# An attention and MLP kernel on one core: slots 1 to 24 by a new order table, with clock-holding matmuls, slots 8 and 9 turned by DMA, and the first hidden units computed part by part

## The chip, the cores and the metric

The kernel runs on one core of a Trainium2 chip. The metric is the device time of one execution in microseconds; lower is better. The engines are named as in the profile: PE is TensorE, with its weight loads as PEld; DVE is VectorE, ACT is ScalarE, POOL is GpSimd, and SP is SyncE, which here only issues DMAs.

## What is computed

```python
# q, k, v: (8, 8, 576, 64) float32; w_in: (512, 2048); w_out: (2048, 512)
scores = q @ k.T / sqrt(64)                       # per batch and head, 576 x 576
kth    = the 32nd largest score of each row
attn   = softmax(where(scores >= kth, scores, -1e9))
x      = (attn @ v) with heads side by side       # 4608 x 512
h      = x @ w_in
out    = (h * sigmoid(1.702 * h)) @ w_out         # 4608 x 512
```

So each of 4608 rows per head pair needs its 32 largest scores, a softmax over these, and the product with v; then each of the 4608 tokens goes through an MLP with 2048 hidden values.

## The kernel before, in words

**Slots.** The work is cut into 144 slots (list `slots`, eighteen for each of eight batches). A slot is 128 rows of queries for a pair of heads; the last 64 rows of two pairs share a slot. Batch 0 has slots 0 to 17: slots 0 to 3 are the four head pairs of the first 128 rows, slots 4 to 7 those of the next, and so on. When the four pairs of one set of rows are through, they make a *block* of 128 tokens for the MLP. For a slot n the steps are:

- PE multiplies queries and keys into PSUM (`scores`, tile s_ps), two slots ahead; there is one set of score banks. ACT copies them out (`copy_scores`, tile sc).
- DVE pairs the two halves of each row as maximum and minimum (`pair_up`, tile ranked), one slot ahead, and finds the 32 largest by four rounds of eight, taking each eight out before the next (`topk`, `find`, tiles top and ranked).
- POOL makes the thresholds (`bounds`, tiles cut and low); ACT masks and exponentiates (`mask`, `exps`, tile pr); POOL and DVE invert the sums (`invert`, tiles some and rden).
- The weights are turned so that the keys lie on partitions (tile pt). In slots 0 to 9 PE does it: POOL scales an identity by the inverse sums (`divide`, tile by), PE multiplies by it in eight full matmuls and two half ones (`turn_main`, `turn_ends`, tile tp), and ACT copies PSUM out in two copies of 128x512 and one of 128x128. From slot 10 on a DMA does it: POOL scales the weights themselves (`normalize`), ACT splits them into 16-bit halves (`split`), SP writes them to DRAM (rows) and reads them back transposed (`turn_by_dma`).
- PE multiplies by v (`values`, later `values_at` and `values_of_two`, tile o), and ACT puts the result in its place in the block (tile xT).

**The MLP.** The 2048 hidden values of a block are cut into four *units* of 512. `hidden` computes one in PSUM: four groups of 128 by four steps of 128 over x, 16 matmuls, where step c needs head pair c of the block. The tile is one of two banks (po) or a borrowed one (ph). `tanh` and `gate` make the activation on ACT and POOL, and `project` multiplies it by w_out into the two banks. The first two blocks are computed whole; the later ones by a Strassen scheme.

**Weights.** 32 pieces of w_in and w_out are loaded by SP into a ring of seven places (`load_piece`, tile raws), and rounded in slots 0 to 10 (`round_piece`): some steps on ACT, a shift on DVE, and a last addition on POOL that frees the place. `may_project` asks whether the pieces that a projection needs have been finished; in slot n those of the slots before n have, which are 3n − 1 pieces. A projection of unit u of a block needs 16 + 4u.

**The order.** `slot(n)` issues slots 0 to 10, `filling_slot(n)` slots 11 to 20, and `steady_pair(n)` pairs of slots from 21 on. The steps of everything up to slot 24 are collected and then issued in the order of a table, `ORDER`, a permutation of their numbers written out in the file (`issue_in_order`; "8 11 0+8" means steps 8, 11 and 0 to 7). Each engine takes its steps strictly in that order. From slot 25 on the steps are issued as the code has them. In the profile a step out of the table has line 133 (L133), one behind it line 131 (L131), since every engine call goes through the helper `Engine`.

**Around the change.** `stay_warm(count)` (line 282) issues matmuls of the identity on itself whose result nobody reads. In slots 1 to 3, as long as no block is ready, `slot` ends with eight of these. The first block is complete when slot 3's values are in place; `bring_all` (line 1050), called in slot 5, brings them and issues the first unit, and `hidden` at the end of slots 5, 6 and 7 the other three. From slot 8 on `slot` projects one unit at its end if more than two wait and their weights are there. Slots n from 4 on turn slot n − 1 at their end and multiply it by v at once.

Of the kernel before, what the change touches and what calls it, by code (L numbers as in the profile page):

```python
# [19 lines left out]
P = 128  # L20
# [125 lines left out]
def kernel(  # L146
# [43 lines left out]

    FIRST = (TAIL, 0)
    MAIN = (0, NF + 1)
    SCALE = 1.0 / float(D) ** 0.5


    PROJECTS = 7


    TURNS = 4
    SETTLED = 10  # L200
    PAIRED = SETTLED + 1
    STEADY = PAIRED + 2
# [1214 lines left out]
```

## Time and profile before

| | |
|---|---|
| median of 3 runs | 1366.73 us |
| lowest and highest | 1366.28, 1373.02 us |
| the profiled execution | 1371.88 us |
| its span, first to last instruction | 1370.1 us |
| mean granted TensorE clock | 0.995 |
| busy: PE, DVE, ACT, POOL | 1340.9, 1274.6, 1166.2, 978.4 us |

The profile is of one execution. The span is shorter than that execution by 1.8 us around it. A busy engine is one that has an instruction in flight; for PE the ends of matmuls are modelled, and a matmul in 32-bit floating point shows as two records. The idle time before an instruction is put down to what released it last. The DVE and PE are called late or early here by the time at which they issue their first step behind the table.

### The profile page before, as it was taken

What the parts mean: (1) busy time and instruction counts of PE and PEld (TensorE: products, weight loads), DVE (VectorE), ACT (ScalarE), POOL (GpSimd) and SP (SyncE); (2) the same over time, 40 slices, a digit from 0 to 9 for tenths busy, and PEclk for the clock granted to TensorE, in tenths of its full rate; (3) what the DMA queues carried; (4) which work ended last, traced back from release to release, by engine and by line L of the source; (5) the groups of instructions that cost most, each with busy time, mean ns of one, the idle gap of its engine ahead of it and who ended that gap; (6) DMA issues with size and microseconds to landing.
All of it is one profiled execution on the core that took longest, in us unless ns stands there. A gap on an engine that the chain in (4) does not pass through costs nothing.

```text
span 1370.1 us, 54342 instructions
## 1 busy us (share of the span) xinstructions
PE 1340.9 (98%) x22532; PEld 1202.3 (88%) x22532; DVE 1274.6 (93%) x3374; ACT 1166.2 (85%) x1936; POOL 978.4 (71%) x1782
## 2 busy tenths in 40 slices
PE   7899999999999999999999999999999999999998
PEld 5687588999989998999999999999998999999998
DVE  7999999999999999999999999999999999999912
ACT  6999898998889979898889888998988888888841
POOL 3888887777767776777777777777777777777770
PEclk9899999999999999999999999999999999999999
DMA  8443759677998767988899796988899767765540
GB/s 233 144 146 110 177 155 212 170 191 195 217 211 212 183 150 203 209 200 197 206 208 206 181 195 164 237 192 196 204 202 202 192 172 181 186 148 135 143 122 17
DMA packets 527223, 246.92 MB, mean 180 GB/s; under 512 B 458880, under 2 KB 505472, under 8 KB 526976
## 3 DMA queue, kind: packets, MB, share of 16 engines
q1 hardware_dynamic: 526544, 243.16, 72.9%
q8 instruction: 177, 2.90, 0.9%
q14 instruction: 70, 0.57, 0.1%
q10 hardware_dynamic: 432, 0.30, 0.1%
HBM read 46.01 MB, written 103.42 MB: 109 GB/s over the span
## 4 chain that ended last, share of the span: by engine, by line
PE 86%; DMA 4%; DVE 3%; ACT 3%; POOL 1%; SPq 1%; issue 1%; DVEq 0%; ACTq 0%; POOLq 0%
PE ph L131 31%; PE po L131 28%; PE o L131 10%; PE s_ps L131 9%; PE po L133 4%; DMA pt<-rows 2%; DVE ranked L133 2%; PE o L133 1%; DVE top L133 1%; PE s_ps L133 1%; SPq L131 1%; PE ph L133 1%; PE tp L133 1%; ACT sc L133 1%; DMA rows<-sc 1%
## 5 line engine op out<-in xcount | busy, mean ns | idle before, releaser
L131 DVE MAX8 top<-ranked 128x8 f32<-128x288 f32 (+1 forms) x952 | 526.7, 595 | 0.0
L131 PE MATMUL ph<-xT,win 128*64 128x128 f32 x8064 | 464.2, 273 | 0.0
L131 PEld LDWEIGHTS ph<-xT,win 128*64 128x64 f32 x8064 | 441.2, 137 | 25.9 <-issue 21.9
L131 DVE MATCH_REPLACE8 ranked<-top,ranked 128x288 f32<-128x288 f32 x714 | 382.0, 543 | 0.0
L131 ACT COPY sc<-pr 128x2304 uint16<-128x2304 uint16 x120 | 253.7, 2114 | 87.0 <-POOL pr L131 87.0
L131 POOL TENSOR_SCALAR pr<-pr,rden 128x576 f32<-128x576 f32 x240 | 177.3, 749 | 40.0 <-DVE rden L131 40.0
L131 PE MATMUL po<-wout,h 128*64 128x128 f32 x2000 | 194.2, 273 | 0.0
L131 PE MATMUL po<-raws,h 128*64 128x128 f32 x2000 | 194.2, 273 | 0.0
L131 ACT ACTIVATE pr<-sc,low 128x576 f32<-128x576 f32 x240 | 183.4, 770 | 0.2 <-POOL raws L131 0.2
L131 POOL TENSOR_SCALAR some<-den 128x2 f32<-128x2 f32 x120 | 26.7, 222 | 209.8 <-ACT pr L131 209.8
L131 ACT ACTIVATE sc<-sc,cut 128x576 f32<-128x576 f32 x240 | 174.1, 781 | 0.1
L131 DVE TENSOR_TENSOR ranked<-s_ps,sc 128x576 f32<-128x576 f32 x236 | 166.6, 747 | 4.3 <-ACT sc L131 4.3
L131 POOL TENSOR_TENSOR th<-th,h 128x512 f32<-128x512 f32 x123 | 157.7, 1282 | 10.3
L131 PE MATMUL po<-wout,th 128*64 128x128 f32 x2064 | 156.6, 273 | 0.0
L131 ACT COPY sc<-s_ps 128x576 f32<-128x576 f32 x234 | 138.0, 642 | 19.8 <-PE s_ps L131 9.7
L131 PE MATMUL s_ps<-qk_t 64*64 64x288 f32 x1872 | 140.5, 415 | 0.0
L131 PEld LDWEIGHTS po<-wout,h 128*64 128x64 f32 x2000 | 126.4, 137 | 0.0
L131 PEld LDWEIGHTS po<-raws,h 128*64 128x64 f32 x2000 | 126.4, 137 | 0.0
L131 PEld LDWEIGHTS po<-wout,th 128*64 128x64 f32 x2064 | 121.3, 137 | 0.0
L131 PE MATMUL o<-pt,v_l 128*64 128x128 f32 (+1 forms) x2144 | 120.7, 266 | 0.0
L131 PEld LDWEIGHTS o<-pt,v_l 128*64 128x64 f32 x2144 | 106.6, 137 | 9.9 <-issue 9.1
L131 POOL TENSOR_TENSOR h<-th 128x128 f32<-128x128 f32 x248 | 114.1, 460 | 0.3
(121 smaller groups left out, 2216.6 us busy)
## 6 DMA issues: line engine op xcount, KB each, us to landing
rows<-sc SPq DMA_DIRECT2D x134, 576.0 KB, 3.8
qk_rows<-halves SPq DMA_DIRECT2D x24, 576.0 KB, 5.2
out_dram<-raws SPq DMA_DIRECT2D x68, 128.0 KB, 3.6
raws<-in_moe_w_in_dram SPq DMA_DIRECT2D x16, 512.0 KB, 4.7
raws<-in_moe_w_out_dram SPq DMA_DIRECT2D x16, 512.0 KB, 3.7
qk_l<-in_q_dram SPq DMA_DIRECT2D x28, 256.0 KB, 4.2
qk_l<-in_k_dram SPq DMA_DIRECT2D x28, 256.0 KB, 4.4
v_l<-in_v_dram SPq DMA_DIRECT2D x4, 1024.0 KB, 7.5
```

Source lines behind the costliest of these rows:

```text
L131: do(*args, **kwargs)
L133: self.engines.collected.append(lambda: do(*args, **kwargs))
```

## The change

Slots 1 to 3 get three matmuls of `stay_warm` at four places each (slots 2 and 3 at five), in place of eight at the end. Slots 8 and 9 are turned by DMA, as the slots from 10 on are; their values are multiplied one slot later, in slots 10 and 11. The first block's first two units are done part by part: the steps over x of head pairs 0 and 1 at the end of slot 3, into the two banks, and those of head pairs 2 and 3 in slot 5. The block's third and fourth unit follow in slots 5 and 6. Slot 6 gets a second `tanh` and `gate`. Projecting begins in slot 7, and no longer asks for more than two units waiting. The table is new from its first line to its last.

```diff
@@ -33,89 +33,89 @@
 ORDER = """
-8 11 0+8 9 12 10 13+5 22 18 23+2 33 25+2 19 27+5 34 32 20 38+4 35 21 36 97 37 42+4 98 46+4 99 50 54+6 100 53 51
...
-2592 2514+2 2528+2 2516+2 2530+4 2518+6 2534+2 2585+2
+8 11 0+8 9 12 10 13+5 22 18 23+2 33 25 19 26+5 20 31 34 32 21 38+4 97 35+3 98 42+8 99 50 54+2 100 56+4 53 51
...
+2532+2 2583+2
 """
...
@@ -193,10 +193,11 @@
     SCALE = 1.0 / float(D) ** 0.5
 
 
-    PROJECTS = 7
+    PROJECTS = 6
 
 
     TURNS = 4
+    BY_DMA = 8
     SETTLED = 10
     PAIRED = SETTLED + 1
     STEADY = PAIRED + 2
@@ -284,6 +285,10 @@
         none = both_banks[1][:]
         for i in range(count):
             nc.tensor.matmul(none[:, 0:P], lhsT=of, rhs=of, start=True, stop=True)
+
+    def warm(n):
+        if 0 < n < TURNS:
+            stay_warm(3)
 
     def load(name, b, hp, queue=None):
 
@@ -1047,6 +1052,29 @@
 
     put_off = []
 
+    def hidden_part(c, place):
+
+        for g in range(2):
+            for i in range(G):
+                nc.tensor.matmul(
+                    both_banks[g][:, i * P : (i + 1) * P],
+                    lhsT=win[:, c, (g * G + i) * P : (g * G + i + 1) * P],
+                    rhs=xs[:, place, c, :],
+                    start=(c == 0 and i == 0),
+                    stop=(c == CC - 1 and i == G - 1),
+                )
+
+    def bring_parts():
+
+        while put_off:
+            put_off.pop(0)()
+        x = ready[0]
+        for c in range(2, CC):
+            hidden_part(c, x.place)
+        for bank in both_banks:
+            fs, x.left = x.left[:G], x.left[G:]
+            to_gate.append((bank[:], fs, x))
+
     def bring_all():
 
         waiting = len(ready)
@@ -1078,14 +1106,16 @@
         else:
             exponentials(n - 1, bring_all if n % 4 == 1 and n > TURNS + 1 else lambda: None)
             if n == TURNS + 1:
-                pass
-                bring_all()
+                bring_parts()
             copy_scores(n + 1)
             bring_all()
             if 1 < n <= TURNS:
                 turn_main(n - 2)
                 turn_ends(n - 2)
+                warm(n)
             if n > TURNS + 1:
+                tanh(True)
+            if n == TURNS + 2:
                 tanh(True)
             do("size", 3)
             if n == TURNS + 1:
@@ -1099,7 +1129,9 @@
                 if last and n > 2:
                     last["pool_size"]()
             if i == (9 if n < 3 else 7):
-                if n > 0:
+                if n > BY_DMA:
+                    invert(n - 1)
+                elif n > 0:
                     divide(n - 1)
                 if last and n < 3:
                     last["pool_size"]()
@@ -1114,13 +1146,21 @@
                 do("shift", 3)
             if i == (13 if n == TURNS + 1 else 10):
                 gate()
+            if i == 13 and n == TURNS + 2:
+                gate()
+            if i in (2, 6, 11):
+                warm(n)
         bounds(n)
         for piece in some:
             unfinished.extend(piece["finish"][piece is last :])
         if n < NP:
             for fn, args in preparing:
                 fn(*args)
-        if n >= TURNS:
+        if n > BY_DMA:
+            normalize(n - 1)
+            split(n - 1)
+            turn_by_dma(n - 1)
+        elif n >= TURNS:
             turn_main(n - 1)
             turn_ends(n - 1)
         do("low", 3)
@@ -1131,21 +1171,22 @@
             copy_scores(n + 2)
         if n == 0:
             return
-        idle = not ready and n < TURNS
+        warm(n)
         if 1 < n <= TURNS:
             values(n - 2, put_off if n == TURNS else None)
-        if n >= TURNS:
-            values(n - 1, put_off)
+        if n == TURNS - 1:
+            for c in range(2):
+                hidden_part(c, place_of(0, 0))
+        if n >= TURNS and n != BY_DMA + 1:
+            values(n - 2 if n > BY_DMA else n - 1, put_off)
         if n >= NP:
             for fn, args in preparing:
                 fn(*args)
-        if n > PROJECTS and may_project(2):
+        if n > PROJECTS and may_project(0):
             project(n == SETTLED)
-        if idle:
-            stay_warm(8)
         if n == SETTLED:
             turn_qk(1, 0)
-        hidden()
+        hidden(ps_t if n == TURNS + 1 else None)
 
     def dues(n):
 
@@ -1247,7 +1288,7 @@
         unit = lambda: hidden(ps_t)
         th = lambda: tanh(True)
         sums = lambda count: lambda: sum_weights(count)
-        put = lambda: project(True)
+        put = lambda: project(True) if to_project else None
         held = lambda n: lambda: brought.append(values_held(n))
         bring = lambda: brought.pop(0)()
 
@@ -1265,10 +1306,10 @@
 
         gate()
         bring_all()
-        filling_slot(11, [copy_qk], [], [unit], [])
+        filling_slot(11, [copy_qk], [], [lambda: values(BY_DMA + 1, put_off), unit], [])
         finish_all()
         summing.extend(all_weight_sums())
-        filling_slot(12, [th], [sums(1)], [put, put, ends_in_turn], [])
+        filling_slot(12, [bring_all, th], [sums(1)], [put, put, ends_in_turn], [])
         filling_slot(13, [copy_ends, th, leave_all], [gate, sums(1)], [of_qk(1), put, held(13)], [sums(1)])
         filling_slot(14, [copy_qk, bring], [gate, sums(1)], [put, hidden], [sums(1)])
         filling_slot(15, [copy_ends, th], [sums(3)], [put, hidden, of_qk(2)], [gate])
```

163 rows, old and new, of the table ORDER are left out of this document.

## The prediction

> **What bounds the kernel now.** The page first: its span and the busy shares.
>
> ```profile
> span 1370.1 us, 54342 instructions
> PE 1340.9 (98%) x22532; PEld 1202.3 (88%) x22532; DVE 1274.6 (93%) x3374; ACT 1166.2 (85%) x1936; POOL 978.4 (71%) x1782
> ```
>
> PE (TensorE) and DVE are both nearly full. That is a mean over two stages, so I cut the span into windows. The columns are PE, PEld, DVE, ACT and POOL busy, then granted clock, DMA share and GB/s.
>
> ```profile
> 70.00:120.00 50.00, 49.23 (x445) 39.84 (x443) 48.59 (x130) 47.02 (x93) 40.96 (x56) 1.00 0.46 139
> 120.00:230.00 110.00, 104.59 (x1349) 79.59 (x1351) 107.03 (x283) 98.36 (x167) 90.91 (x133) 1.00 0.70 170
> ...
> 600.00:800.00 200.00, 200.00 (x3546) 183.54 (x3546) 197.42 (x522) 181.69 (x294) 144.69 (x277) 1.00 0.84 199
> ```
>
> From 600 to 800 us PE is busy all the time, but from 120 to 230 DVE is fuller than PE, 107.0 against 104.6 us of 110. The chain in order of time, from the first instruction of slot 25 (L131 marks what is issued after the table, L133 what the table orders), shows the late stage; its first row here is an early one, which says when DVE takes up its unbroken work of slot 0:
>
> ```profile
> 15.86 0.75 DVE top L133
> ...
> 253.06 3.06 PE po L131 x56
> 256.12 3.49 PE ph L131 x64
> 259.62 1.13 PE s_ps L131 x16
> 260.75 3.65 PE ph L131 x64
> 264.39 3.06 PE po L131 x56
> 267.45 1.13 PE s_ps L131 x16
> 268.58 2.12 PE o L131 x40
> ```
>
> One pair of slots is 3.06 + 3.49 + 1.13 + 3.65 + 3.06 + 1.13 + 2.12 = 17.64 us of PE without a hole. Nothing behind slot 25 is edited, and the number of hidden units and projections issued before it is the same after the edit as before (below). So the 1117 us from 253.06 to the end stay, and **the question is when PE and DVE reach slot 25.** The DVE timeline gives its side, with its idle time in brackets:
>
> ```profile
> 35.56 0.76 DVE L133 TENSOR_TENSOR ranked<-s_ps,sc 128x576 f32<-128x576 f32 x1 [1.41 <-ACT sc L133]
> ...
> 95.30 0.17 DVE L133 RECIPROCAL rden<-some 128x2 f32<-128x2 f32 x1 [0.69 <-POOL some L133]
> ...
> 177.12 0.17 DVE L133 RECIPROCAL rden<-some 128x2 f32<-128x2 f32 x1 [0.54 <-POOL some L133]
> ...
> 178.68 0.76 DVE L133 TENSOR_TENSOR ranked<-s_ps,sc 128x576 f32<-128x576 f32 x1 [0.97 <-ACT sc L133]
> ...
> 213.76 0.17 DVE L133 RECIPROCAL rden<-some 128x2 f32<-128x2 f32 x1 [1.36 <-POOL some L133]
> ...
> 232.26 0.17 DVE L133 RECIPROCAL rden<-some 128x2 f32<-128x2 f32 x1 [0.89 <-POOL some L133]
> ...
> 248.06 0.80 DVE L131 MAX8 top<-ranked 128x8 f32<-128x288 f32 x2
> ...
> 251.20 1.41 DVE L131 TENSOR_TENSOR ranked<-s_ps,sc 128x576 f32<-128x576 f32 x2
> ```
>
> These are all its holes over 0.5 us between 15.86 us and 248.06, when it starts on slot 25: 1.41 + 0.69 + 0.54 + 0.97 + 1.36 + 0.89 = 5.86 us. A slot takes (248.06 − 15.86) / 25 = 9.3 us, so slot 5 begins near 15.9 + 5 × 9.3 = 62. DVE's own work isn't edited, so its side can come at most **5.9 us** earlier. On the other side PE is late: its scores at 259.62 need the pairing that DVE ends at 251.20 + 1.41 = 252.61, so PE could stand **7.0 us** earlier there with DVE as it is. Together 12.9 us is all that can be won.
>
> **The change part by part.** PE's waits in the same stretch, from its timeline; then the prices of PE work from the chain, and three windows with their clock:
>
> ```profile
> 28.95 1.19 PE L133 MATMUL s_ps<-qk_t 64*64 64x288 f32 x2 [6.37 <-DVE ranked L133]
> ...
> 52.63 3.78 PE L133 MATMUL tp<-by,pr 128*128 128x128 f32 x16 [2.85 <-POOL by L133]
> ...
> 154.83 1.09 PE L133 MATMUL o<-pt,v_l 128*64 128x128 f32 x16 [1.02 <-DMA pt<-rows]
> ...
> 173.37 1.09 PE L133 MATMUL o<-pt,v_l 128*64 128x128 f32 x16 [1.09 <-DMA pt<-rows]
> ```
>
> ```profile
> 70.70 3.83 PE po L133 x32
> ...
> 97.55 1.78 PE tp L133 x16
> ...
> 100.01 0.39 PE tp L133 x4
> ```
>
> ```profile
> 20.00:30.00 10.00, 3.63 (x26) 2.62 (x24) 10.00 (x31) 9.59 (x20) 7.25 (x10) 0.87 0.92 306
> 30.00:40.00 10.00, 10.00 (x81) 6.87 (x80) 8.59 (x21) 7.83 (x13) 8.79 (x9) 0.79 0.54 169
> ...
> 50.00:60.00 10.00, 7.37 (x46) 5.51 (x47) 10.00 (x27) 8.55 (x17) 8.78 (x13) 0.66 0.48 157
> ```
>
> Two records stand for one matmul here, so 3.83 us for x32 is one unit of 16 matmuls, 0.24 us each.
>
> *Clock-holding matmuls.* Slot 1 gets 12 in place of 8, slots 2 and 3 get 15 each in place of 8: 18 more, 4.3 us. *First units by parts.* The 16 matmuls of head pairs 0 and 1 go from slot 5 to slot 3: 3.8 us more there, 3.8 us less in slot 5. Together 8.1 us come onto PE before 62 us. The cover is PE's waits of 6.37 and 2.85 us (9.2), and the clock: 0.13, 0.21 and 0.34 of three 10 us windows were withheld, 6.8 us. I cost this at nothing; if the cover fails in slot 3, where 7 × 0.24 + 3.8 = 5.5 us meet a wait of 2.85, scores 5 come 2.7 us later.
>
> What the clock brings is little: DVE was full in two of the three windows, and in the middle one had the hole of 1.41 us. [...]
>
> *Slots 8 and 9 turned by DMA.* PE loses 1.78 + 0.39 = 2.2 us for each, 4.4 in all. In their place stand normalizing on POOL, the split on ACT, and two transfers. First groups of the whole span and two issue rows from the page, then groups and issues of 72 to 140 and 90 to 200 us, last SP's own timeline:
>
> ```profile
> L131 ACT COPY sc<-pr 128x2304 uint16<-128x2304 uint16 x120 | 253.7, 2114 | 87.0 <-POOL pr L131 87.0
> L131 POOL TENSOR_SCALAR pr<-pr,rden 128x576 f32<-128x576 f32 x240 | 177.3, 749 | 40.0 <-DVE rden L131 40.0
> ...
> L131 ACT COPY sc<-s_ps 128x576 f32<-128x576 f32 x234 | 138.0, 642 | 19.8 <-PE s_ps L131 9.7
> ...
> rows<-sc SPq DMA_DIRECT2D x134, 576.0 KB, 3.8
> ```
>
> ```profile
> L133 ACT COPY pt<-tp 128x512 f32<-128x512 f32 x11 | 6.3, 596 | 0.5 <-PE tp L133 0.5
> ...
> L133 POOL TENSOR_SCALAR by<-ident,rden 128x128 f32<-128x128 f32 x10 | 3.6, 373 | 0.7 <-PE o L133 0.4 <-DVE rden L133 0.4
> ...
> L133 ACT COPY pt<-tp 128x128 f32<-128x128 f32 x6 | 1.6, 267 | 0.5 <-PE tp L133 0.5
> ```
>
> ```profile
> pt<-rows SPq DMA_TRANSPOSE x7, 5.2
> ```
>
> ```profile
> 93.66 33.78 SPq L133 DMA_DIRECT2D raws<-in_moe_w_out_dram  x8
> ```
>
> For a slot, ACT does one copy of 2.11 us and not two of 0.60 and one of 0.27: 0.6 us more. POOL does 2 × 0.75 and not 2 × 0.37: 0.75 us more. For two slots that is 1.3 us of ACT and 1.5 of POOL at about 100 to 120 us; from 70 to 120 ACT was busy for 47.0 and POOL for 41.0 of 50 us. The tile comes through POOL 1.5 + ACT 2.1 + 3.8 + 5.2 = 12.6 us and not 0.75 + 2.2 + 1.5 = 4.4; the value products of slots 8 and 9 are put one slot later, a slot of 9.3 us, so 8.2 more fits, by 1.1 us. The new wait is PE's for this tile; scores stand behind it.
>
> *The rest.* An extra tanh and gate in slot 6 are those of slot 8, one unit earlier: moved, not added. Projecting starts in slot 7 and not 8, but the second projection needs weight pieces that slot 8 doesn't have yet, so slots 7, 9 and 10 project in place of 8, 9 and 10: three, as before. The eight hidden units of the first two blocks are through by slot 11, as before. The new table reorders everything up to slot 24. Nothing in the trace prices it; I bound it by the holes above (up to 12.9 gained) and by a loss as large as the new waits (about 9, below), and take nothing by itself.
>
> **The sum.** PE is rid of 3.8 + 4.4 = 8.2 us between 62 and 253. Not all of it counts: at 154.83 and 173.37 PE waits for tiles of slots that DMA turns, so it is paced by DVE, POOL and ACT there, and being early means waiting longer, but projections that now run behind these waits can run in them. I take the two waits as filled: 1.02 + 1.09 = 2.1 us. Of DVE's holes those ahead of slot 11 lie where the clock and the lighter PE act: 1.41 + 0.69 = 2.1 us. The later four are waits for POOL and ACT, which get no less work; they stay. So **4.2 us** are won. The profiled execution took 1371.88 us (span 1370.1 and 1.8 around it), 5.2 above the median of 1366.73; from its own time 1367.7, and against the median **1362.5 us**. The forecast's own range is a gain of 2 to 8 us, 1358.7 to 1364.7.
>
> **The rivals.** *PE was the path (gain 8 to 12.9).* All 8.2 us come off, since the table finds other PE work for the waits: 1358.5, at most 1353.8. For it: PE stands 7.0 us late at slot 25, so DVE would not stop it at once. Against it: PE's waits at 154.83 and 173.37. A form of it: were PE the path in slots 1 to 4 too, the withheld clock would bring 6.8 and not 1.4 us there, 5.4 on top of the 4.2, or 1357.1; one chance in twenty, because DVE is full there. [...]
>
> *The DMA turn comes too late (slower).* SP takes its steps in order, and the table leaves the write of slot 8's tile behind the last weight loads. These eight hold SP from 93.66 to 127.44, waiting for places in the ring that POOL frees. A write then lands at 131.2 and the tile at 136.4; slot 8's values stand on PE behind scores 13, with scores 14 behind them. DVE wants scores 14 in slot 13, about 15.9 + 13.5 × 9.3 = 141.4; with PE's scores (1.13) and two ACT copies (2 × 0.64) they must start by 139. So it decides when the tile lands after 139, 2.6 us later than I work out; slot 9 repeats it, and slots 10 and 11 queue behind both. If each of the two comes a transfer later (5.2), less the 2.6 of room once, that is 7.8 us, and with the 1.3 us of ACT about 9: 1375.9 without any gain.
>
> *It does nothing.* DVE hides it all, the holes only move: 1366.7, ±2.
>
> **How the numbers follow.** Forecast 0.42, PE was the path 0.26 (0.05 of it for the clock), too late 0.24, nothing 0.08. I predict 1362.5. The range 1354 to 1375 takes in the forecast, the first rival to its bound, and nearly half of the slower one; about 0.15 is left out. A measurement of this kernel can tell about 0.5%, 6.8 us. Faster by more: the first rival and the forecast's upper end, 0.26 + 0.07 = 0.33. Slower by more: 0.22 of the slower rival. Within: 0.45.
>
> **What would show it.** Right: slot 25 (the first L131) begins on PE near 249 and on DVE near 246; the hole of 1.41 us near 35 gone; clock 1.0 from 20 to 60; PE's waits for the turned tile about 155 and 173 gone or no longer, and nothing but 17.6 us pairs after. The first rival: PE at slot 25 by 245. The slower one: PE waiting for the turned tile between 125 and 145, with a DVE hole at the pairing behind it. I am wrong altogether if the pairs after slot 25 change, or if the distance from slot 25 to the end isn't 1117 us within 2.

## The result, and the profile after

The changed kernel takes 1363.78 us (median of 10 runs, 1360.74 to 1365.16), the kernel before 1371.22 (median of 10, 1366.28 to 1373.57, its first three runs among them). The ratio is 0.9946, with a 95% interval from 0.9931 to 0.9962: 7.4 us or 0.54% faster. The profiled execution took 1363.19 us.

First the page of the changed kernel, its span and busy shares.

```profile
span 1361.4 us, 54339 instructions
PE 1340.3 (98%) x22528; PEld 1200.6 (88%) x22528; DVE 1274.6 (94%) x3374; ACT 1167.5 (86%) x1932; POOL 979.5 (72%) x1782
```

The busy times are those of before within 1.7 us; the span is 8.7 us shorter. So what went are waits, and the question is where. The chain of waits in order of time (start, length, engine, tile, line) shows the late slots and the first pair behind the table.

```profile
172.04 0.50 ACT ob L133
172.59 0.33 PE po L133
...
190.08 6.38 DMA pt<-rows
...
196.60 0.69 PE o L133 x16
...
246.06 3.06 PE po L131 x56
249.12 3.50 PE ph L131 x64
252.61 1.13 PE s_ps L131 x16
253.74 3.64 PE ph L131 x64
257.39 3.06 PE po L131 x56
260.44 1.13 PE s_ps L131 x16
261.57 2.12 PE o L131 x40
```

From the first L131 row on everything is as it was: the pair of slots adds up to the same 17.64 us, and from 246.06 to the end it is 1115.3 us, where it was 1117.0. But slot 25 begins 7.0 us earlier. And from 172.59 us on the chain is PE, but for one copy on ACT of 0.71 us and one transfer of 6.38 us. In the kernel before the same view runs over PE too, from 61.88 to 100.40 us, and with two transfers and some 5 us on ACT from 154.83 to 213.63; but there it leaves PE once more, for 18 us of ACT, DVE and POOL, and comes back to it only at 231.82:

```profile
61.88 2.58 PE o L133 x40
...
100.01 0.39 PE tp L133 x4
...
173.37 1.09 PE o L133 x16
...
213.66 1.19 ACT sc L133 x2
...
230.94 0.77 ACT pr L133 x2
...
231.82 0.45 PE o L133 x13
```

DVE's timeline of the changed kernel, with idle time in brackets, gives the other side: its three largest holes, the last one (at 234.56), and the first search of slot 25.

```profile
31.63 0.76 DVE L133 TENSOR_TENSOR ranked<-s_ps,sc 128x576 f32<-128x576 f32 x1 [0.50 <-ACT sc L133]
...
81.87 0.76 DVE L133 TENSOR_TENSOR ranked<-s_ps,sc 128x576 f32<-128x576 f32 x1 [1.00 <-ACT sc L133]
...
220.49 1.42 DVE L133 TENSOR_TENSOR ranked<-s_ps,sc 128x576 f32<-128x576 f32 x2 [1.09 <-ACT sc L133]
...
234.56 0.17 DVE L133 RECIPROCAL rden<-some 128x2 f32<-128x2 f32 x1 [0.16 <-POOL some L133]
...
242.56 0.80 DVE L131 MAX8 top<-ranked 128x8 f32<-128x288 f32 x2
```

Read these with the rows of before. The four late holes of before (177.12, 178.68, 213.76, 232.26; 3.76 us) are now 1.25 us. The hole near 35 has shrunk from 1.41 to 0.50. Near 82 there is a new one of 1.00.

DVE's time can be added up exactly, whichever engine leads: it reaches slot 25 at its first search, plus its work, plus its holes; PE follows at some distance. (DVE is the fuller engine from 120 to 230 us, with 107.03 against 104.59 us in the kernel before and 108.91 against 106.06 in the changed one; from 70 to 120 PE is, in the kernel before with 49.23 against 48.59 us, in the changed one with 49.56 against 48.26.) The table does that for every profiled execution of this study (us; "holes" is the sum of all brackets on DVE's timeline from its first search to slot 25, "PE" the first L131 row on PE's timeline, or the line that takes its place; that row can lie up to 0.2 us ahead of the piece in the chain; each ratio is to runs of the kernel before made beside it).

| kernel | first search | from there to slot 25 | of it holes | PE behind DVE | PE at slot 25 | ratio of times, 95% |
|---|---|---|---|---|---|---|
| before | 12.04 | 236.02 | 6.88 | 4.84 | 252.90 | 1 |
| before_again | 12.07 | 238.32 | 8.95 | 4.86 | 255.25 | 0.9982 (0.9966 to 0.9997) |
| changed | 10.69 | 231.87 | 3.43 | 3.33 | 245.89 | 0.9946 (0.9931 to 0.9962) |
| no_warm | 11.00 | 232.30 | 2.30 | 3.34 | 246.64 | 0.9935 (0.9915 to 0.9955) |
| parts_late | 10.68 | 232.62 | 3.97 | 3.34 | 246.64 | 0.9937 (0.9917 to 0.9956) |
| turn_pe | 10.97 | 237.29 | 8.35 | 3.34 | 251.60 | 0.9986 (0.9974 to 0.9999) |
| old_tail_new | 11.61 | 235.47 | 6.32 | 3.33 | 250.41 | 0.9966 (0.9951 to 0.9982) |
| dve_more | 11.36 | 235.86 | 4.26 | 3.34 | 250.56 | 0.9961 (0.9947 to 0.9976) |
| pe_more | 11.93 | 232.73 | 4.17 | 3.34 | 248.00 | 0.9929 (0.9906 to 0.9951) |
| copies_first | 12.11 | 231.23 | 2.46 | 3.33 | 246.67 | 0.9928 (0.9909 to 0.9948) |
| old_new_table | 10.79 | 250.57 | 20.61 | 3.33 | 264.69 | 1.0064 (1.0048 to 1.0080) |
| all_old_table | 11.13 | 259.01 | 27.13 | 4.86 | 275.00 | 1.0137 (1.0124 to 1.0150) |
| warm_only_old | 11.77 | 250.52 | 20.37 | 4.61 | 266.90 | 1.0084 (1.0071 to 1.0097) |
| dma_only_old | 11.59 | 246.56 | 15.83 | 4.66 | 262.81 | 1.0059 (1.0045 to 1.0074) |

For the change itself the 7.0 us on PE at slot 25 are: 1.35 earlier start, 3.45 fewer holes, 0.70 less time in DVE's work, and 1.51 less distance from DVE to PE. Of these the first is most likely chance (the last section), and the 0.70 is less than DVE's work differs between traces: the stretch without its holes takes 228.4 to 231.9 us where DVE has the same steps. Against the second trace of the kernel before, before_again, the same sum is 9.36 us: 1.38, 5.52, 0.93 and 1.53. So the holes are the largest item, at 3.4 to 5.5 us, and the distance is the steadiest.

### The profile page after: what moved, and what is told of

It reads as the page before. It is cut to its first block, busy times and chain, and to the rows that moved or that the text cites. A ratio compares the mean times of both kernels' runs of the same rounds, so it can differ in the third digit from the quotient of the medians.

```text
span 1361.4 us, 54339 instructions
## 1 busy us (share of the span) xinstructions
PE 1340.3 (98%) x22528; PEld 1200.6 (88%) x22528; DVE 1274.6 (94%) x3374; ACT 1167.5 (86%) x1932; POOL 979.5 (72%) x1782
## 4 chain that ended last, share of the span: by engine, by line
PE 89%; DVE 5%; ACT 3%; DMA 1%; issue 1%; POOL 1%; SPq 0%; DVEq 0%; ACTq 0%; POOLq 0%
PE ph L131 33%; PE po L131 29%; PE o L131 10%; PE s_ps L131 10%; PE po L133 3%; DVE ranked L133 3%; DVE top L133 2%; PE ph L133 2%; PE s_ps L133 1%; PE o L133 1%; DMA pt<-rows 1%; ACT sc L133 1%; PE tp L133 1%; ACT pr L133 0%; ACT raws L133 0%
## 5 line engine op out<-in xcount | busy, mean ns | idle before, releaser
L131 DVE MAX8 top<-ranked 128x8 f32<-128x288 f32 (+1 forms) x952 | 526.9, 596 | 0.0
L131 PE MATMUL ph<-xT,win 128*64 128x128 f32 x8064 | 464.3, 273 | 0.0
L131 PEld LDWEIGHTS ph<-xT,win 128*64 128x64 f32 x8064 | 441.3, 137 | 25.9 <-issue 22.4
L131 DVE MATCH_REPLACE8 ranked<-top,ranked 128x288 f32<-128x288 f32 x714 | 382.0, 543 | 0.0
L131 ACT COPY sc<-pr 128x2304 uint16<-128x2304 uint16 x120 | 253.6, 2113 | 84.6 <-POOL pr L131 84.6
L131 POOL TENSOR_SCALAR pr<-pr,rden 128x576 f32<-128x576 f32 x240 | 177.2, 749 | 37.4 <-DVE rden L131 37.4
L131 PE MATMUL po<-raws,h 128*64 128x128 f32 x2000 | 194.3, 273 | 0.0
L131 PE MATMUL po<-wout,h 128*64 128x128 f32 x2000 | 194.3, 273 | 0.0
L131 ACT ACTIVATE pr<-sc,low 128x576 f32<-128x576 f32 x240 | 183.0, 767 | 1.4 <-DMA qk_rows<-halves 1.4
L131 POOL TENSOR_SCALAR some<-den 128x2 f32<-128x2 f32 x120 | 26.7, 222 | 210.3 <-ACT pr L131 210.3
L131 ACT ACTIVATE sc<-sc,cut 128x576 f32<-128x576 f32 x240 | 173.8, 778 | 0.1
L131 DVE TENSOR_TENSOR ranked<-s_ps,sc 128x576 f32<-128x576 f32 x236 | 166.6, 748 | 0.2 <-ACT sc L131 0.2
L131 POOL TENSOR_TENSOR th<-th,h 128x512 f32<-128x512 f32 x123 | 157.7, 1282 | 10.3
L131 PE MATMUL po<-wout,th 128*64 128x128 f32 x2064 | 156.5, 273 | 0.0
L131 ACT COPY sc<-s_ps 128x576 f32<-128x576 f32 x234 | 137.9, 642 | 16.3 <-PE s_ps L131 11.8
L131 PE MATMUL s_ps<-qk_t 64*64 64x288 f32 x1872 | 140.5, 415 | 0.0
L131 PEld LDWEIGHTS po<-wout,h 128*64 128x64 f32 x2000 | 126.5, 137 | 0.0
L131 PEld LDWEIGHTS po<-raws,h 128*64 128x64 f32 x2000 | 126.5, 137 | 0.0
L131 PEld LDWEIGHTS po<-wout,th 128*64 128x64 f32 x2064 | 121.3, 137 | 0.0
L131 PE MATMUL o<-pt,v_l 128*64 128x128 f32 (+1 forms) x2144 | 120.7, 266 | 0.0
L131 PEld LDWEIGHTS o<-pt,v_l 128*64 128x64 f32 x2144 | 106.6, 137 | 9.9 <-issue 9.1
L131 POOL TENSOR_TENSOR h<-th 128x128 f32<-128x128 f32 x248 | 114.0, 460 | 0.3
```

The lines of the kernel that those rows point to most:

```text
L131: do(*args, **kwargs)
```

## The experiments

Three theories were put before the runs. A: DVE's work and its holes set the time up to slot 25. B: PE sets it, with its clock and its work one to one. C: the new order makes the gain, whatever the named parts do. The chains above already warn that A can't hold for the whole stretch: they run over PE for 30 to 40 us between 60 and 100 in both kernels, and in the changed one from 172.59 us to the end.

### How far two runs of one kernel differ

before_again is the kernel before, unedited.

> The kernel before once more, unchanged, for a second trace of it. All theories: the same time as before within 0.2%. In question is the opening: in the first trace DVE began its first search at 12.04 us, in the changed kernel's at 10.69, though nothing in the opening was edited. If that is chance, this trace has another start between 10.5 and 12.5 us and its first step behind the table moves with it; if it belongs to the kernel, 12.0 again.

It came out at 0.9982 (0.9966 to 0.9997): an interval that doesn't quite reach 1 for the same program. Steps below about 0.2% are therefore not read from the times here, only from the traces. The traces differ too: behind 170 us DVE's holes are 5.85 us here and 3.76 in the first trace. And the first search came at 12.07 us, as in the first trace; by the test that the expectation set, that speaks for a start that belongs to the kernel. The last section weighs it against the other traces.

### The clock-holding matmuls taken out

```diff
     def warm(n):
-        if 0 < n < TURNS:
-            stay_warm(3)
+        pass
```

The table is the changed kernel's, without these 42 steps (two neighbouring steps far behind them also change places).

> The changed kernel without any of the clock-holding matmuls of slots 1 to 3 (42 left out, and the 24 of before are not put back); the rest of the table as it is. Work that nobody reads is left out. Theory A (DVE and its holes set the time up to slot 25, PE has room in slots 1 to 4): the clock falls below 0.9 between 20 and 60 us, the hole of DVE near 32 us grows by about 1 us, and the time is 0 to 2 us above the changed kernel, 5 to 7 under the one before. [...] Theory C (the new order makes the gain, whatever the parts): no difference to the changed kernel, 7 under before.

1363.0 us, 0.9935 (0.9915 to 0.9955): not slower than with them. The windows show that the clock was indeed withheld. Columns as in the prediction; first the changed kernel, then no_warm.

```profile
20.00:30.00 10.00, 6.75 (x46) 4.60 (x43) 10.00 (x29) 9.29 (x19) 8.80 (x10) 0.84 0.98 346
30.00:40.00 10.00, 9.02 (x77) 6.83 (x74) 9.50 (x29) 9.57 (x19) 8.23 (x13) 0.93 0.52 166
```

```profile
20.00:30.00 10.00, 4.42 (x20) 1.78 (x20) 10.00 (x29) 8.37 (x18) 8.57 (x10) 0.60 1.00 343
30.00:40.00 10.00, 7.54 (x55) 5.73 (x52) 9.98 (x31) 9.28 (x19) 8.44 (x13) 0.72 0.52 178
```

Without them the granted clock is 0.60 and 0.72, and DVE's column (the third) is 10.00 and 9.98: fuller than with them, since the hole at 31.63 isn't there; theory A had expected it to grow by about 1 us, a miss. Granted clocks of 0.60 and 0.72 on PE, behind a full DVE, cost nothing that these times show; the matmuls bring nothing measurable to this kernel.

### The first units not part by part

The 16 matmuls of head pairs 0 and 1 are moved in the table from slot 3 to just ahead of those of pairs 2 and 3; nothing else is edited.

> The changed kernel with its table altered in one place: the 16 matmuls of the first two hidden units over head pairs 0 and 1 stand right ahead of those over pairs 2 and 3, not in slot 3. Theory A: PE takes 3.5 to 3.8 us more near 62 us, but DVE is not held up by that for more than 1 us; 0 to 2 us above the changed kernel. Theory B (PE's work in the fill counts one to one): 3.5 us above it. Theory C (order): between these, as the order around it was made for the parts being early.

1362.86 us, 0.9937 (0.9917 to 0.9956): no loss, and in the trace PE is at slot 25 within 0.75 us. The early part, left out by itself, brings nothing measurable either.

### Slots 8 and 9 turned by PE, in the new order

```diff
-    BY_DMA = 8
+    BY_DMA = 10
...
-        filling_slot(11, [copy_qk], [], [lambda: values(BY_DMA + 1, put_off), unit], [])
+        filling_slot(11, [copy_qk], [], [unit], [])
...
-        filling_slot(12, [bring_all, th], [sums(1)], [put, put, ends_in_turn], [])
+        filling_slot(12, [th], [sums(1)], [put, put, ends_in_turn], [])
```

The steps of the turn stand in the table where the DMA's stood.

> The changed kernel with slots 8 and 9 turned by PE as before (20 matmuls, six copies on ACT, four scalings on POOL, their values one slot earlier in the code), set into the new table at the places of the normalizing and the split. Theory A: ACT gets 1.2 us and POOL 1.5 us less, PE 4.4 us more, all beside a full DVE: within 2 us of the changed kernel. Theory B: 4.4 us above it. Theory C: 0 to 4 us above it, by what the misfit of table and steps costs.

1369.32 us, 0.9986 (0.9974 to 0.9999). Against no_warm and parts_late, measured beside it, that is 6.3 to 6.5 us more, and nearly the whole gain is gone. All three theories missed it: A had within 2 us, C up to 4, and B with its 4.4 comes nearest. DVE's timeline has two holes that the changed kernel doesn't have:

```profile
121.31 0.17 DVE L128 RECIPROCAL rden<-some 128x2 f32<-128x2 f32 x1 [1.62 <-POOL some L128]
...
134.30 0.17 DVE L128 RECIPROCAL rden<-some 128x2 f32<-128x2 f32 x1 [3.51 <-POOL some L128]
```

Follow the second one back: POOL's sum waited for ACT's exponentials (pr),

```profile
134.04 0.22 POOL L128 TENSOR_SCALAR some<-den 128x2 f32<-128x2 f32 x1 [4.27 <-ACT pr L128]
```

and ACT had stood in front of copies whose source PE hadn't made yet, for 2.12, 1.83 and 1.25 us:

```profile
125.85 0.75 ACT L128 COPY pt<-tp 128x512 f32<-128x512 f32 x2 [2.12 <-PE tp L128]
...
131.10 0.27 ACT L128 COPY xT<-o 128x128 f32<-128x128 f32 x1 [1.83 <-PE o L128]
...
132.61 0.59 ACT L128 COPY pt<-tp 128x512 f32<-128x512 f32 x1 [1.25 <-PE tp L128]
```

So the loss comes through ACT's waits for PE ahead of the exponentials. Whether these come from the place of the copies in ACT's queue or from PE's 4.4 us of matmuls, which make PE late for them, this run doesn't separate. For the second: in turn_pe PE has no wait over 0.5 us from 104 to 137 us, and the changed kernel leaves PE little room there (its windows, columns as in the prediction):

```profile
70.00:120.00 50.00, 49.56 (x417) 35.61 (x417) 48.26 (x129) 47.52 (x91) 43.38 (x57) 1.00 0.46 151
120.00:170.00 50.00, 48.61 (x433) 31.84 (x431) 50.00 (x131) 47.84 (x81) 43.89 (x59) 1.00 0.78 183
```

That is 1.8 us of 100, less than the 4.4. For the first: pe_more, below, has 2.4 us more of PE at about the same time and hardly loses. The loss is tied to this order: the kernel before turns both slots by PE, and its holes nearest to that place are 0.69 us (95.30) and less.

### Parts and orders crossed

all_old_table has the steps of the changed kernel in the order of the old table, warm_only_old the kernel before with the new warm matmuls, dma_only_old the kernel before with the DMA turn of slots 8 and 9, both in the old order; old_new_table has the steps of the kernel before in the order of the new table. Steps that a table doesn't have stand behind the step that they follow in the other.

> All three parts of the change in the order of the old table: each step that both kernels have stands where the old table has it, new ones stand at the places of those that they replace (normalizing and split where the PE turns were) or behind the step that they follow in the new table (clock-holding matmuls, values of slots 8 and 9). So the early partial units stand where the old table had them, mostly in slot 5. Theory A and B (the parts make the gain): at least half of the 7.4 us is kept, 4 us or more under before. Theory C (the order makes it): within 2 us of before, or slower.

> The kernel before in its old table with one part of the change: the 42 clock-holding matmuls at their new places in place of 24. Theory A: the clock is back near 1 from 30 to 60 us and the DVE hole of 1.41 us near 35 shrinks; 0 to 2 us under before. Theory B: 4 to 7 us under before. Theory C: no difference.

> The kernel before in its old table with one part of the change: slots 8 and 9 turned by DMA, their values one slot later. Theory A: within 2 us of before. Theory B: 4.4 us under before. My rival of a turn that comes too late: PE waits for the turned tile between 125 and 145 us, 3 to 9 us above before.

> The steps of the kernel before in the order of the new table, with the PE turns of slots 8 and 9 at the places of the normalizing and the split, and the 24 clock-holding matmuls at the places of the first eight in each of slots 1 to 3. Theory A and B: within 3 us of before. Theory C: 4 us or more under before, most of the gain.

All four are slower than the kernel before, by 8 to 19 us, with 16 to 27 us of holes on DVE. For old_new_table that misses all theories: A and B had it within 3 us of the kernel before, C at 4 us or more under. But three of them, those in the old order, don't price the parts. The timelines of warm_only_old, PE, then ACT, then DVE, show why:

```profile
150.44 12.79 PE L129 MATMUL po<-wout,th 128*128 128x512 f32 x26
```

```profile
163.71 0.58 ACT L129 COPY qk_t<-tp 128x512 f32<-128x512 f32 x1 [9.16 <-PE tp L129]
```

```profile
36.57 0.76 DVE L129 TENSOR_TENSOR ranked<-s_ps,sc 128x576 f32<-128x576 f32 x1 [2.69 <-ACT sc L129]
...
169.99 0.17 DVE L129 RECIPROCAL rden<-some 128x2 f32<-128x2 f32 x1 [7.38 <-POOL some L129]
```

My way of carrying the order over has put 13 matmuls of projection in one run ahead of a transpose, and all three kernels have such a run of 12 to 13 us and a hole of 6.8 to 7.7 us behind it. That is the edit's fault and not the parts'. What they do show: 12.8 us of PE in the wrong place became a wait of 9.16 us on ACT and 7.38 us on DVE. And the hole near 36, where the warm matmuls are, is 2.69 us with the new ones in the old order and 1.41 without. old_new_table has no such run; its holes are largest at 87.31 (4.59 us), 102.09 (5.93) and 147.05 (3.51), probably where the new order expects units and turned tiles earlier than the old steps make them; no run shows that. So the whole new order doesn't suit the old steps, and what the parts are worth in the old order stays unmeasured. dma_only_old is as slow as my rival of a late turn had it, but no wait of PE for a turned tile stands between 125 and 145 us, which was its sign.

### Extra work on DVE, and on PE

```diff
+        again = {...}
         for i in order:
-            steps[i]()
+            for _ in range(1 + again.get(i, 0)):
+                steps[i]()
```

dve_more repeats four searches of slot 10, pe_more the transposes of slot 10, 20 more in all.

> The changed kernel with the four 576-wide searches of slot 10 done a second time each on DVE (four MAX8 of 128x576, about 0.72 us each by the row `110.18 1.40 DVE ... x2`, so 2.9 us more of DVE's work; the result is the same). Theory A, DVE's work and holes set the time up to slot 25: DVE and PE both come to slot 25 about 2.9 us later (DVE near 245.5 in place of 242.56), and the time is about 2.9 us above the changed kernel's, a ratio near 0.997 to the kernel before. Theory B, the PE sets it one to one: slot 25 stays on PE within 1 us, ratio 0.994 to 0.9955. Theory C, only the order of the new table as it was fitted counts: anything between.

> The changed kernel with the eight transposes of slot 10 repeated, 20 more in all (four of them took 0.60 us at 110.61, so 2.6 to 3.0 us more of TensorE's work; the result is the same). Theory A, DVE sets the time up to slot 25 and PE has room between the slots: 0 to 1 us, ratio 0.994 to 0.995, DVE at slot 25 within 1 us of 242.56. Theory B, the PE one to one: 2.6 to 3.0 us, ratio near 0.9965, with DVE's holes grown as it waits for scores. Theory A falls if this costs as much as the kernel with more searches.

DVE's timeline of dve_more, one repeated search beside its first:

```profile
112.76 1.53 DVE L133 MAX8 top<-ranked 128x8 f32<-128x576 f32 x2
```

PE's timeline of pe_more, 16 transposes and then 12, where the changed kernel has 4 (in 0.60 us) and 4:

```profile
112.35 1.91 PE L133 MATMUL tp<-ident,qk_l 128*128 128x128 f32 x16
...
129.55 1.53 PE L133 MATMUL tp<-ident,qk_l 128*128 128x128 f32 x12
```

The stretch from DVE's first search to slot 25 grew by 3.99 us in dve_more (235.86 against 231.87): 3.16 of work and 0.83 of holes, of which 0.60 is the hole near 32, ahead of the edit. In pe_more it grew by 0.86, of which 0.61 lies in that same early hole, though PE was busy for 2.4 us more (1342.7 against 1340.3). The times, side by side on one chip: 1368.03 us for dve_more, 1363.87 for pe_more. At slot 10 DVE's work counts in full, as far as the scatter tells, and 2.4 us of PE's hardly at all: theory A there, and B is out for slot 10. Neither kernel has extra work between 60 and 100 us or behind 172, where the chain is PE.

### The late order alone

old_tail_new has all steps of the kernel before (its 24 warm matmuls among them), and its order up to the first search of slot 14; from there on, where both kernels have the same steps, the order of the new table.

> The kernel before with all its own steps (no warm matmuls in slot 1 to 4, no turn by DMA, first units as before) and its own table up to the first search of slot 14; behind that point, where both kernels have the same steps, the order of the new table. It holds none of the three parts that the change names. If the order of the late slots is worth what the traces gave it (holes at 177.12, 178.68, 213.76 and 232.26 smaller by about 2.5 us, PE 3.3 in place of 4.7 to 5.0 us behind DVE at slot 25, 1.5 us): PE reaches slot 25 about 4 us earlier than in the kernel before, ratio 0.997. If the gain needs the parts or the steps ahead of it: ratio 1.000, or above it because the old head and the new tail do not fit.

1368.8 us, 0.9966 (0.9951 to 0.9982), as expected if the order counts (0.997). DVE's timeline:

```profile
150.87 0.17 DVE L128 RECIPROCAL rden<-some 128x2 f32<-128x2 f32 x1 [2.36 <-POOL some L128]
...
225.01 1.42 DVE L128 TENSOR_TENSOR ranked<-s_ps,sc 128x576 f32<-128x576 f32 x2 [1.15 <-ACT sc L128]
...
239.09 0.17 DVE L128 RECIPROCAL rden<-some 128x2 f32<-128x2 f32 x1 [0.16 <-POOL some L128]
...
247.08 0.80 DVE L126 MAX8 top<-ranked 128x8 f32<-128x288 f32 x2
```

Behind 170 us only 1.31 us of holes are left of 3.76, and the distance to PE is 3.33 in place of 4.84: 2.45 and 1.51 us, the 4 us that were expected. The hole of 2.36 us at the seam between the two orders takes back most of the first. So PE is at slot 25 2.5 us before the kernel before and 4.8 before its second run. The times say 4.7 us (2.5 to 6.7) against the kernel before, but only about 2 against before_again, whose interval overlaps. The late order brings something without any of the named parts; how much lies between 2 and 5 us.

The other traces bear it out. Behind 170 us DVE's holes are 0.22 to 1.31 us in all nine with the new late order. With the old one they are 2.6 to 5.9 us in four traces and 12.2 in the fifth, all_old_table, where a hole of the misplaced projections (6.81) is among them.

### Three copies moved ahead

In copies_first, three of ScalarE's copies of scores stand earlier in the table: one ahead of an exponential near 80 us, two ahead of the two masks near 218.

> The changed kernel with three of ScalarE's copies of scores put ahead of the work that stood before them in its queue: one ahead of an exponential near 80 us, two ahead of the two masks near 218 us, which waited 0.58 us for POOL's cut. They end DVE's two largest holes (81.87 with 1.00 us, 220.49 with 1.09 us). Theory A: DVE reaches slot 25 by 1 to 1.8 us earlier than in the changed kernel and PE with it, ratio near 0.9935, too small a step to be told from the changed kernel by the times alone, so read it from the trace. Rival: the holes come back later because the exponentials and POOL's sums behind the copies are 0.6 to 1.2 us later; then slot 25 stays where it is or is later.

DVE's timeline now has these for the holes near 82 and 220:

```profile
82.51 0.76 DVE L128 TENSOR_TENSOR ranked<-s_ps,sc 128x576 f32<-128x576 f32 x1 [0.24 <-ACT sc L128]
83.58 0.17 DVE L128 RECIPROCAL rden<-some 128x2 f32<-128x2 f32 x1 [0.31 <-POOL some L128]
...
235.34 0.17 DVE L128 RECIPROCAL rden<-some 128x2 f32<-128x2 f32 x1 [0.22 <-POOL some L128]
```

Both are gone, 2.09 us, but the stretch to slot 25 is only 0.64 us shorter (231.23). Some came back as smaller holes (0.55 at 82.51 and 83.58, 0.35 at 159.05), and the distance to PE stayed at 3.33. Near 220 the chain of the changed kernel is PE, so a hole on DVE there probably has little worth. With 1364.55 us the times can't tell it from the changed kernel: a miss for theory A's 1 to 1.8 us.

## Why the prediction was right, and where it wasn't

The time forecast was 1362.5 us and it is 1363.78. That is closer than the reasoning deserves. The forecast of a gain of 4.2 was taken off 1366.73, the median of three runs; over ten runs the kernel before is at 1371.22. The base was 4.5 us too low, the gain 3.2 too small, and the two nearly cancel. The gain of 7.4 lies within the forecast's own range of 2 to 8. Of the chances, the 0.45 for within 0.5% didn't come true; the 0.33 for faster by more did, by a hair.

**What bounds the kernel: right in part.** The stretch from slot 25 stayed as it was (1115.3 us, within the 2 allowed, and 17.64 us a pair). At slot 10 DVE is the limit, as dve_more against pe_more shows. What I hadn't seen is that the limit changes hands within the table: the chain of the kernel before runs over PE from 61.88 to 100.40 us and for most of 154.83 to 213.63, and in the new order PE leads from 172.59 us. The prediction's own row of 70 to 120 us said so, with PE at 49.23 and DVE at 48.59.

**The later four holes: wrong; this is the step that failed.** It read "they stay", since POOL and ACT get no less work, and of the table: "Nothing in the trace prices it"; it was taken at nothing. The holes went from 3.76 to 1.25 us with the work of POOL and ACT up by 1.1 and 1.3 us, and in old_tail_new, where no part is changed, to 1.31. So these waits hang on where a step stands in its engine's queue, and the order of the queues was the largest item of the edit. The trace did bound it: the brackets say what a better order can win at most, and I took nothing of them by an argument about amounts of work.

**PE's distance to DVE: right as a bound, not counted in the sum.** The 7.0 us by which PE could stand earlier "with DVE as it is" weren't won that way; the distance to DVE fell by 1.51. On PE's timeline of before these are two waits,

```profile
225.09 0.44 PE L133 MATMUL po<-wout,th 128*64 128x128 f32 x4 [0.25 <-ACT raws L133]
...
231.82 0.45 PE L133 MATMUL o<-pt,v_e 64*64 64x64 f32 x14 [0.92 <-ACT pr L133]
```

1.17 us in all, both for ACT, and probably the larger share of the 1.51; the changed kernel's last wait is earlier:

```profile
196.60 0.69 PE L133 MATMUL o<-pt,v_l 128*64 128x64 f32 x16 [1.27 <-DMA pt<-rows]
```

The distance is 3.33 or 3.34 in all nine traces with the new late order, and 4.61 to 4.86 in the five with the old one.

**PE's two waits at 154.83 and 173.37 filled, 2.1 us: the waits went, their worth isn't shown.** PE no longer waits for turned tiles there, as forecast; what waits it has there are for ACT (0.88 us at 153.82, 0.70 at 172.59, 0.58 at 174.74). In the kernel before the chain runs over both transfers, so the waits may have had a worth. But no run adds or takes PE work at that place alone, and the 7.0 us are added up on DVE without them; what they brought isn't shown.

**DVE's early holes, 2.1 us: 0.9 of it.** The hole of 1.41 shrank to 0.50. The one of 0.69 is now 0.38, and with the new one of 1.00 at 81.87 the holes between 60 and 120 us have not come down (1.71 before, 1.68 after). Even the 0.9 is one draw: in the traces that have the changed kernel's steps and order up to there the hole near 32 is anything from none (turn_pe) to 1.11 us (pe_more).

**The warm matmuls and the early parts at nothing: right,** with no_warm and parts_late. The clock did not come back as forecast (0.84 and 0.93 from 20 to 40 us, 1.00 from 40 on); it didn't matter. That all of the 6.8 us withheld would come back, on which the forecast of the clock and the 5.4 us in one form of the first rival count, was my estimate, and no run shows it. From 20 to 30 us the granted clock is 0.60 without the warm matmuls, where PE is busy for 4.42 of 10 us; with them it is 0.84 in the changed kernel, but 0.63, 0.69 and 0.72 in dve_more, pe_more and copies_first, which have the same matmuls there. DVE is busy for 10.00 of the 10 us in all five, and the clock had no worth that the times show. That form of the rival is out.

**The DMA turn: amounts right, worth open.** ACT's busy time rose by 1.3 us as worked out, POOL's by 1.1 (1.5 forecast). I counted it as 4.4 us off PE, of which only a part was to count. In the new order taking it back costs 6.3 to 6.5 us, through ACT's queue, which then stands before copies that wait for PE (turn_pe); how much of that is the 4.4 us on PE isn't shown.

**The rivals.** "PE was the path" needed slot 25 by 245; it began at 246.06, and pe_more speaks against it at slot 10, while the chains speak for it between 60 and 100 us and behind 172, and turn_pe came nearest to it: half right, and not ruled out for the stages that no run tested. The slower rival, that the DMA turn comes too late, rested on weight loads that hold SP until 127.44. SP's timeline after:

```profile
87.83 25.47 SPq L133 DMA_DIRECT2D raws<-in_moe_w_out_dram  x7
116.29 0.35 SPq L133 DMA_DIRECT2D rows<-sc  x1
```

In the new order the loads let SP go at 113.30, so the write and the transpose of slot 8's tile aren't behind them, and no wait of PE for that tile shows between 111 and 150 us. I had carried SP's old order into the new kernel, the same fault as with the holes.

What stays open: of the 3.45 us of holes, about 2.5 are the late order's and 0.9 lie in the hole near 35, which scatters as much by itself; the holes in between trade places, and no run separates which step of the table closed which. The 1.7 us by which the changed kernel was also faster behind slot 25 in the profiled pair aren't the change's: nothing is edited there, and over the fourteen traces that stretch varies from 1112.7 to 1117.2 us.

## What to carry to other kernels

A wait for an engine that isn't full can be a question of order and not of amount: bound a new order by the brackets of the waits that it can move, not by the work that stays the same. Ask at each stage which engine leads, since an order can hand the lead to another one: extra work in one slot, once on each engine, tells it in two runs, for that slot. And take a forecast off a base as well measured as the effect: three runs were 4.5 us off, more than the forecast gain.

## What the runs showed of the hardware

The first search on DVE came at 10.68 to 12.11 us, though the steps ahead of it are the same in every kernel but for small shifts in their order. The groups of PE in the window up to 7.4 us, for before, the changed kernel and copies_first (busy us, then mean ns of one), show where that starts:

```profile
L133 PE MATMUL tp<-ident,qk_l 128*64 128x128 f32 x20 | 2.4, 425 | 0.0
```

```profile
L133 PE MATMUL tp<-ident,qk_l 128*64 128x128 f32 x20 | 1.3, 278 | 0.0
```

```profile
L128 PE MATMUL tp<-ident,qk_l 128*64 128x128 f32 x20 | 2.4, 426 | 0.0
```

The first 20 transposes take 1.3 to 2.4 us, and the first search moves with them; copies_first has the changed kernel's opening, step for step, and has the long one. dve_more and pe_more, with the same opening too, lie between, with means of 331 and 412 ns and the first search at 11.36 and 11.93 us. The granted clock reads 1.00 in this window in the kernel before and in the changed one, beside means of 425 and 278 ns for the same instruction, so the difference doesn't show in it; what makes it, no trace shows. Both traces of the kernel before have the late start (12.04 and 12.07 us), so by themselves they would let it be the kernel's; but the start varies within either opening, from 11.13 to 12.07 us in the traces with the old order there and from 10.68 to 12.11 with the new. So 1.35 us of the 8.7 between the two profiled spans are most likely chance and not change.
